# A recurrence and an MLP mixer on one core: another written-out order for all engines

## The chip, the core and the metric

The kernel runs on one core of a Trainium2 chip. The metric is the device time of one execution in microseconds (us). Before the change it is 173.35 us, the median of 3 runs (172.86 to 173.45). The engines are PE (TensorE), DVE (VectorE), ACT (ScalarE), POOL (GpSimd) and SP (SyncE).

## The reference

For each of 4 batches and 8 heads of 48 channels a gated recurrence runs over 768 steps. Its output, with the heads side by side (768 x 384), goes through an MLP mixer: first over the steps (token weights), then over the channels.

```python
f = 1.0 / (1.0 + np.exp(-f_logit))
for t in range(S):                       # S = 768
    state = f[:, :, t, :, None] * state + np.einsum('bhd,bhe->bhde', k[:, :, t], v[:, :, t])
    y[:, :, t] = np.einsum('bhd,bhde->bhe', q[:, :, t], state)
x = y.transpose(0, 2, 1, 3).reshape(B, S, H * D)
xt = x.transpose(0, 2, 1)
h = np.maximum(xt @ w_tok1, 0.0) @ w_tok2
u = x + h.transpose(0, 2, 1)
out = u + np.maximum(u @ w_ch1, 0.0) @ w_ch2
```

w_tok1 is 768 x 256, w_tok2 256 x 768, w_ch1 384 x 1536 and w_ch2 1536 x 384. All inputs and the output are float32; the kernel multiplies in bfloat16.

## The kernel before

**The recurrence by chunks.** The 768 steps of a batch are six chunks of 128. A name such as "sums 1 3" is the operation for batch 1, chunk 3. For each chunk ACT computes the logarithm of f from the loaded logits ("exp", "ln", L371 and L372); the logarithm is kept as a high bfloat16 part and a low part ("lo", L379, on DVE or POOL). PE sums both along the steps with a triangular matrix ("sums", L461 and L462). ACT takes the exponential of the sums both ways ("G", "Gi"), DVE multiplies q and k by them ("gated", L490), PE turns the products ("turn", L500), and DVE or ACT copies them out of PSUM ("turned"). PE multiplies them ("scores", L413), DVE masks the result ("masked", L541), and PE forms the part of the state that the chunk adds ("parts", L429). "tsum" and "state" (L577 for the decay) bring the state from one chunk to the next, and "spread" casts it to bfloat16 in two halves (L277 on ACT, L281 on POOL), which "y" of the next chunk multiplies (L560), before its own part within the chunk (L564). Batch 0 works by pairs of chunks instead, on a layout of its own: scores at L676, the masks at L706, "within" at L719, and y with the old state at L743; y 0 5 is the last of these.

**The mixer.** "tok1" (L757) takes the six chunks of x times w_tok1, "h1T" is its ReLU, "tok2" (L773) multiplies by w_tok2, and DVE adds x ("u"). u is turned, by PE ("ut" and its copy "uT") in batches 0 and 1 and by a transposing DMA of SP in batches 2 and 3. "ch1" (L826, three products of 384 columns) takes w_ch1, whose two halves are two tiles; "zT" is its ReLU on ACT (L357) or DVE (L359); "ch2" (L845, three groups of four products for each 128 rows) takes w_ch2; DVE adds u ("sum", L851) and SP stores.

**Loads.** SP loads f of batch 0. All other loads of q, k, v, f and the weights are DMAs that POOL issues (L266 and L272), among its arithmetic and in its row's order.

**What sets the order.** All operations of the four batches are first made as a list of some 1,050, each with what it needs. Then `Plan.run` walks the string ORDER and issues them in this order, so ORDER fixes the row of every engine. A number is an operation; a letter behind it chooses the engine where there is a choice (A for ACT, D for DVE, G for POOL); a number behind a colon chooses the PSUM bank, of which there are eight. `w512` and `w128` are idle products in float32, and `s11` is eleven idle products of 64 columns in bfloat16; their results are not used:

```python
if token[0] in "zsw":
    idle(int(token[1:]), {"z": 512, "s": 64, "w": 0}[token[0]])
    continue
...
op = self.ops[int(token)]
op.engine = engine or op.engines[0]
```

The text speaks of these numbers: 206 is y 0 5, 204 y 0 4, 358, 366, 394 and 402 are the sums of chunks 0 to 3 of batch 1, 208 to 213 and 215 to 220 the tok1 products of batch 0, 344 and 347 the low parts of chunks 1 2 and 1 3, 161 and 199 within of chunks 0 2 and 0 4, 170 and 201 the states 0 3 and 0 4, 62, 81 and 354 the loads of f for batches 1, 2 and 3, 46 and 47 the halves of w_ch1, and 48 w_ch2.

Of the kernel before, what the change touches and what calls it, by code (L numbers as in the profile page):

```python
# [33 lines left out]


ORDER = """
w512 w512 w512 s11 32 0G 6G 33 8G 20D 9D 5G 34 13D 7G 1 21G 35 2 24A 23A 27D 3A 37 26A 29D 14D 28 49 17D 36 19D 51 22G
38 50 53D 54 12D 39 52D 25D 55 100:0 15G 40 58 105:1 56D 57D 102 59 10G 137:2 104 41 11D 30D 107 114:3 60D 142:4 101 42
110 106 108 31A 103 62 119:1:0 139 18D 109 115 145 61D 111:5 143 112 125 144 180:6 141 138 147 113A 116D 43 151:2 146
126A 130 118:3:4 140 44 127A 117:5:1 123 182 152 175:0 153A 4G 122 45 121 176 131G 148:3 120 177 149 64 156:4:2 183 181  # L40
178 124:0:5 150A 162 63 184 186:6 179 187 185 132A 134 47 128D 154:3:4 188A 189:1 158 190 133G 191D 163G 66 157 165A
# [5 lines left out]
296:5 346 362 278:0 275A 347D 370 304:3 351 273D 277A 372:1 365D 279A 280:2 349 297D 298:0 271A 373D 350G 402:4 290:6
305D 75 292:5 281D 291A 374:3 299D 293A 78 375:6 352 376:2 386 403 286:5 76 377 404 284:6 378 79 264:0 258:7 379 285D 77
381A 262:3 259D 265A 282:6 263A 81 399 382:7 283A 300:0 385 287A 400:3 387 380A 302:5 407 405 384D 391:2 406 408:4 80
401D 393A 431:1 301A 409D 260:6 353G 303A 388D 410:0 261A 412:5 383A 414 411:6 389G 392A 268:7 415 434 413 266:2 435  # L50
390A 423 294:0 269A 419:3 416G 267D 433 462:7 87 439:6 424 420A 422 469:2 470 441 463 417G 288:5 421A 418G 432 464 83
471 289D 428:3 295A 311:1 429D 82 316:0 425D 430A 436 90 440 317 426A 442 318 85 472 312 86 313 93 465 437:6 314 91
443:3 319 438A 321:1 320 444D 96 447:0 445:5 99 446:4 448 322 450 427G 331:6 449 97 306:0 457 590 84 587 458 454:5 323
588 451G 455D 584 332 452G 324 585 453G 326:4 92 466 459:1 589G 327 460A 586G 328 89 467 473 474 468A 610:3 475D 461A
307 593 329 479:2 611 476:4 612 480 482:1 456A 485:7 477 596 481G 488:2 483 478A 308 94 486 594 602:1 489 484G 491:7 604
615 496:4 88 498:2 605 494:5 333 499D 497D 606 595G 613 495D 616:2 492 512:5 490G 487A 309 646:7 603 354 334 500:0 524:3
647 617D 513A 508:6 607 501A 510:5 591 525D 502:0 493A 608:1 511D 592G 599 506:3 503D 609D 504:0 95 528:5 507A 505D 509A
638:4 529D 597 522:0 639 618:5 598G 523D 640 619:6 648 620:3 630 98 641 534:0 623 544:6 629 642 600 625G 520:4 624G 614
545A 621 355 530:2 649 631 514:1 622 521A 675:7 531A 651 516:3 515A 643 518:2 601D 356 536:1 519A 635:4 677 537D 526:2
517A 535A 644:1 676 626:3 645D 652:0 628A 550:5 627A 527D 559:6 653D 632G 551A 678 683:2 634G 633G 656:5 679 818 655:7  # L60
659 654:3 684 650 560 660G 685 658 830 661G 542:2 667 662A 538:3 636A 666 637A 561 680 824 672:4 821 686 554:0 833 657
539A 552:7 668 831 673D 663:3 540:5 562 681:1 541A 713:6 819 714 682D 687:5 664A 555 820G 553A 688D 674A 556 669G 665A
357 834 691:4 557 689:3 671A 690:7 543A 693 564:0 827 692 670A 715 836:3 822 694 706:2 698:1 702 695G 548:4 699D 835G
696A 707 708 701 825 565 697G 839 700D 823G 532:7 840 837 716 703:1 533D 838 709 549D 546:5 704D 717 569:4 705D 710 718
843:1 719D 711 570 846 547D 712D 574:6 847 845 826D 844 720:2 828 841 723:5 729:1 848 870:3 721 829G 849 726:7 871 575
727 722G 735:2 724 842 732:7 736 725A 566 730 728A 737G 877:2 872 733 738 576 880 734G 912:7 731A 832G 571 873 739 852:1
572 878 579:5 567 879 905:4 855 330 882 580 857A 881 577 856G 913 874 581 863 914 875 851:1:6 582 850:7:2 907 886:0 876
861 756:5 864D 742:3 862 865G 762:6 743A 853 760:1 906 889 908 867:3 854 764:2 883 866A 780:4 757A 765D 890G 768:7 761A
763D 892G 772:2 310 910 769A 583 858:6 891A 758:1 335 773A 746:7 868A 315 859A 740:2 568 747D 781A 909 766:5 898 860A
741D 325 919:4 759A 899G 885:0:7 767A 884:6:2 897 776:1 888 754:5 750:0 887 784:6 751A 896 744:2 869A 785D 893:7 777D  # L70
902:3 911 901G 778:6 755D 900G 782:1 745D 779A 915 770:5 903A 573 894A 941:6 916 942 752:2 771A 786:0 753D 943 934:5 922
787A 748:2 783D 923G 944 813:0 749D 924G 904D 925G 935 774:2 895D 936 937 775A 803:7 917:2:3 918:1:4 921 804 929 805 920
808:4 806 926:3 930 809 927A 931:1 945 814 932A 946 938 939 947D 793:7 940A 928D 933A 810 954:1 963:3 960:5 964 957:6
788:2 965A 958 948:3 811 959G 789 961 949 951:4 962G 798:5 952 950A 967 799 955 794 956G 953G 795 966 800 815 812 790
807 563 1008:1 1014:4 1002:3 1015D 998:6 801 1003A 1004:4 791 988:5 816 1005A 992:2 999D 990:4 796 968:6 989D 797 991A
1010:7 1009A 802 993A 972:4 558 792 974:1 973D 817 1000:2 1011D 578 984:4 1001A 982:7 975A 994:2 978:1 996:5 979D 980:0
# [839 lines left out]
```

## Time and profile before

| | |
|---|---|
| median of 3 runs | 173.35 us (172.86 to 173.45) |
| the profiled execution | 173.47 us |
| its span (first to last instruction in the trace) | 171.7 us |
| mean granted clock of TensorE | 0.996 |
| loads and stores | 22.72 MB in DMA packets, 132 GB/s over the span |

In a row of the profile stand the start, the busy time, the engine, the line of kernel.py, the operation, what it writes and reads with the shapes, how many instructions it groups, and in brackets the engine's idle time ahead of it with what ended that. PE's product of 384 columns reads as some 0.326 us, but the products overlap, and one starts every 0.163 us. The issue of a load on POOL is a row of POOL; its landing is read from the DMA rows, whose last number is the time from issue to landing.

### The profile page before, as it was taken

Reading aid. Unit: us, or ns where it says so; the run is one execution under the profiler, and the core shown is the slowest. Engines: PE = TensorE matmul, PEld = TensorE weight load, DVE = VectorE, ACT = ScalarE, POOL = GpSimd, SP = SyncE. Lnnn points to the kernel's source line nnn. Section 1 sums busy time; section 2 is a strip of 40 time slices with the busy share of each in tenths; the row PEclk is TensorE's granted clock in tenths of the full one; section 3 lists DMA queues with packets and bytes.
Section 4 is the critical chain, followed back from the end, with each engine's and each line's share of the span. In section 5 each row is a group of like instructions: output and inputs, shape, how many; then the busy total and the mean of one; then the engine's idle time right before and its main releaser. Section 6 shows DMA issues by size and latency. Waiting matters only on the chain.

```text
span 171.7 us, 4436 instructions
## 1 busy us (share of the span) xinstructions
PE 162.2 (94%) x1753; PEld 103.2 (60%) x1753; DVE 123.3 (72%) x262; ACT 105.9 (62%) x240; POOL 90.8 (53%) x131
## 2 busy tenths in 40 slices
PE   6998688999999989999999999999999999999991
PEld 3476565666766645666757665565766656566660
DVE  5589986899995662999777889696976380754051
ACT  5999869995995615979898844959441420542000
POOL 8999678959959598897841933411220031000000
PEclk9999999999999999999999999999999999999998
DMA  5999999999999999969999190978370008250024
GB/s 143 226 171 223 202 196 189 185 144 171 185 196 188 148 139 52 56 83 214 106 143 79 8 130 7 189 166 239 111 168 4 0 7 242 96 211 0 0 96 181
DMA packets 89572, 22.72 MB, mean 132 GB/s; under 512 B 82288, under 2 KB 88736, under 8 KB 89552
## 3 DMA queue, kind: packets, MB, share of 16 engines
q0 software_dynamic: 69600, 13.77, 92.6%
q1 hardware_dynamic: 19952, 8.69, 19.1%
q8 instruction: 13, 0.21, 0.5%
q14 instruction: 7, 0.06, 0.1%
HBM read 25.17 MB, written 4.72 MB: 174 GB/s over the span
## 4 chain that ended last, share of the span: by engine, by line
PE 74%; POOL 11%; DMA 7%; ACT 3%; issue 2%; DVE 1%; POOLq 0%; DVEq 0%
PE ps L826 27%; PE ps L845 24%; DMA f_sb<-in_f_logit_dram 7%; PE ps L757 4%; PE ps L773 4%; POOL qk_sb L266 4%; PE ps L500 3%; PE ps L413 3%; POOL v_sb L266 2%; PE ps L564 2%; PE ps L429 2%; PE ps L461 2%; PE ps L462 2%; PE ps L560 1%; PE ps L811 1%
## 5 line engine op out<-in xcount | busy, mean ns | idle before, releaser
L826 PE MATMUL ps<-uT,w_ch 128*128 128x384 bf16 x288 | 52.6, 326 | 0.0
L845 PE MATMUL ps<-w_ch,zT 128*128 128x384 bf16 (+2 forms) x300 | 52.6, 320 | 0.0
L357 ACT ACTIVATE zT<-ps 128x384 bf16<-128x384 f32 x55 | 25.2, 491 | 21.5 <-PE ps L826 21.1
L845 PEld LDWEIGHTS <-zT 128*128 128x128 bf16 x300 | 27.7, 98 | 17.0
L826 PEld LDWEIGHTS <-w_ch 128*128 128x128 bf16 x288 | 26.8, 97 | 16.3
L359 DVE TENSOR_SCALAR zT<-ps 128x384 bf16<-128x384 f32 x41 | 21.4, 552 | 13.0 <-PE ps L826 12.6
L541 DVE TENSOR_TENSOR AmT<-ps,tri_bf 128x512 bf16<-128x512 f32 x36 | 23.4, 684 | 2.6 <-PE ps L413 2.4
L851 DVE TENSOR_TENSOR x_nat<-x_nat,ps 128x384 f32<-128x384 f32 (+2 forms) x25 | 12.8, 533 | 11.3 <-PE ps L845 11.1
L379 POOL TENSOR_TENSOR Llo<-L 128x384 bf16<-128x384 f32 x15 | 12.4, 834 | 11.8 <-ACT L L372 11.7
L266 POOL DMA_DIRECT2D qk_sb<-in_q_dram x16 | 15.7, 986 | 2.9 <-DMA f_sb<-in_f_logit_dram 2.3
L266 POOL DMA_DIRECT2D v_sb<-in_v_dram x16 | 15.8, 990 | 2.7 <-DMA f_sb<-in_f_logit_dram 1.7
L266 POOL DMA_DIRECT2D qk_sb<-in_k_dram x16 | 15.8, 990 | 0.0
L281 POOL CAST u_bf<-x_nat 128x384 bf16<-128x384 f32 x10 | 5.0, 508 | 14.6 <-issue 10.1
L277 ACT ACTIVATE x_bf<-ps 128x384 bf16<-128x384 f32 x15 | 7.0, 486 | 8.8 <-PE ps L564 8.8
L281 POOL CAST state_bd<-state 48x192 bf16<-48x192 f32 x22 | 8.0, 363 | 8.0 <-PE ps L560 3.0
L757 PE MATMUL ps<-x_bf,w_tok 128*128 128x384 bf16 x48 | 11.9, 326 | 0.0
L789 DVE TENSOR_TENSOR x_nat<-x_nat,ps 128x384 f32<-128x384 f32 x21 | 10.5, 546 | 1.6 <-PE ps L773 1.6
L490 DVE TENSOR_TENSOR qk<-qk_sb,GG 128x768 bf16<-128x768 bf16 x18 | 10.8, 615 | 0.0
L577 POOL TENSOR_TENSOR state<-tsum,glast 128x192 f32<-128x192 f32 x9 | 4.6, 507 | 10.4 <-PE ps L826 4.9
L471 ACT ACTIVATE GG<-ps 128x384 bf16<-128x384 f32 x18 | 8.9, 492 | 1.9 <-PE ps L462 1.0
L371 ACT ACTIVATE f_sb<-f_sb 128x384 f32<-128x384 f32 x18 | 9.1, 524 | 1.3 <-DMA f_sb<-in_f_logit_dram 1.2
L372 ACT ACTIVATE L<-f_sb 128x384 f32<-128x384 f32 x18 | 9.5, 526 | 0.2
(101 smaller groups left out, 264.3 us busy)
## 6 DMA issues: line engine op xcount, KB each, us to landing
out_dram<-x_nat SPq DMA_DIRECT2D x23, 192.0 KB, 2.4
f_sb<-in_f_logit_dram POOLq DMA_DIRECT2D x3, 1152.0 KB, 11.9
f_sb<-in_f_logit_dram SPq DMA_DIRECT2D x3, 384.0 KB, 4.0
qk_sb<-in_q_dram POOLq DMA_DIRECT2D x12, 96.0 KB, 7.7
qk_sb<-in_k_dram POOLq DMA_DIRECT2D x12, 96.0 KB, 7.2
w_ch<-in_moe_w_ch_dram POOLq DMA_DIRECT2D x2, 576.0 KB, 12.8
v_sb<-in_v_dram POOLq DMA_DIRECT2D x12, 96.0 KB, 7.5
w_ch<-in_moe_w_ch_dram POOLq DMA_DIRECT2D x1, 1152.0 KB, 10.4
```

The source lines that it names most:

```text
L266: lambda eng=eng, into=into, of=of: eng.dma_start(out=into, in_=of),
L281: nc.gpsimd.tensor_copy(out_, in_)
L357: nc.scalar.activation(out_, in_, AF.Relu, bias=0.0, scale=1.0)
L359: nc.vector.tensor_scalar(out_, in_, 0.0, None, ALU.max)
L379: op.fn = lambda: (nc.vector if op.engine == DVE else nc.gpsimd).tensor_tensor(lo, full, hi, ALU.subtract)
L490: add(("gated", b, c, *names), DVE, lambda n=n: nc.vector.tensor_tensor(qk[it][:, n, :, 0:D], qk_sb[nb][:, n, :, c, :], GG[i][:, n], ALU.m ...
L541: add(("masked", b, c, p), DVE, lambda half=half, made=made: nc.vector.tensor_tensor(half, made(), tb4, ALU.mult), need=["tri_bf"], make=[ ...
L757: add(("tok1", b, rt, kt), PE, lambda rt=rt, kt=kt, pm=pm: nc.tensor.matmul(banks[pm.at][:, 0:DM], lhsT=w_tok1[:, kt, rt * 128:(rt + 1) * ...
L789: nc.vector.tensor_tensor(to, un, banks[pm.at][:, 0:DM], ALU.add)
L826: nc.tensor.matmul(banks[pm.at][:, 0:384].rearrange("p (n t) -> p n t", t=128), lhsT=w[:, kt, c0:c0 + 128], rhs=uT[:, rows3, kt, :], start ...
L845: nc.tensor.matmul(banks[pm.at][:, 0:n1 - n0], lhsT=zT[:, kt, tt * 128:(tt + 1) * 128], rhs=w_ch2[:, kt, n0:n1], start=(kt == 0), stop=(kt ...
L851: add(("sum", b, tt, n0), DVE, lambda un=un, pm=pm, n=n1 - n0: nc.vector.tensor_tensor(un, un, banks[pm.at][:, 0:n], ALU.add), make=[("x_n ...
```

## The change

Only the string ORDER is replaced. The operations, what they compute and the code that makes them stay. The new order differs from the first line to the last; its first lines and those around the sums of batch 1 read:

```diff
-w512 w512 w512 s11 32 0G 6G 33 8G 20D 9D 5G 34 13D 7G 1 21G 35 2 24A 23A 27D 3A 37 26A 29D 14D 28 49 17D 36 19D 51 22G
...
-193:3:6 136A 169 155:1:4 135A 164G 197 67 192:2:5 159 46 160 336 195 w512 w128 161:4:6 170G 337 196 339 338G 173 198 340
-166 194:2 172A 341G 199:5:1 129A 200 171A 68 174A 204 201D 358:0 342 167D 208:2 203A 209 202G 205D 215:3 359 65 206 210
-361 211 207D 216 212 217 343 213 218 219 214D 360 220 344G 366:7 168D 221A 242 238 369 230:2 69 231 222:4 223 232 367
...
+w512 w512 w384 s19 32 20G 7G 33 8D 6G 10D 0D 34 11G 19D 1 5D 9G 2 24D 3A 27D 23A 18D 21G 22G 35 49 37 50 16G 51 36 52D
...
+129A 169 193:1:5 164A 160 135A 47 128D 165A 192:4:6 159 339 65 336 197 161:2:0 337 170G 195 340 166 338G 198 342 194:5
+173 172A 196 171G 358:1 343 341G 200 199:6:7 360 167D 359 201G 215:5 136D 204 361 216 203G 366:4 205D 202G 208:3 362
+174A 217 68 363 209 206 367 210 168D 364:1 369 67 207D 211 218 345 212 365D 213 66 219 220 214A 374:2 221D 368 242 72
...
```

- **Idle products.** Before: three w512 and eleven small ones at the start, and w512 and w128 between the scores 0 4 and within 0 2. Now: two w512, one w384 and nineteen small ones at the start, and none later.
- **Engines.** DVE has 281 operations instead of 261, ACT 225 instead of 239, POOL 121 instead of 127. The ReLU copies zT stand at 48 on ACT and 48 on DVE instead of 55 and 41, the casts x_bf at 6 and 18 instead of 15 and 9, the low parts at 13 on DVE and 11 on POOL instead of 9 and 15, and the casts of the state at 16 on ACT and 24 on POOL instead of 18 and 22.
- **Rows.** Every engine's row has another order, the loads on POOL too. y 0 5 (206) now stands behind five tok1 products (208, 209, 215, 216, 217) and the sums of 1 0 and 1 1 (358, 366); before it stood behind three (208, 209, 215) and the sums of 1 0.

POOL's row shows the three places that the prediction speaks of. The first is the end of the startup. Before, the row goes from the load of q 1 1 to the cast of state 0 4; state_95 is the state, Llo_79 the low parts, w_ch10_66 and w_ch11_67 the halves of w_ch1.

```order
L266 DMA qk_sb1_70<-in_q_dram 128x8x48
L272 DMA w_ch10_66<-in_moe_w_ch1_dram 128x3x768
L577 TENSOR_TENSOR state_95<-tsum_96,gpair1_121 128x192
L379 TENSOR_TENSOR Llo_79<-L1_78 128x8x48 x2
L266 DMA v_sb1_73<-in_v_dram 128x8x48
L281 CAST state_bd0_97<-state_95 48x4x48
```

Now, from the first half of w_ch1 on, with the load of v 1 0 ahead of state 0 3:

```order
L272 DMA w_ch10_66<-in_moe_w_ch1_dram 128x3x768
L272 DMA w_ch11_67<-in_moe_w_ch1_dram 128x3x768
L266 DMA v_sb1_73<-in_v_dram 128x8x48
L577 TENSOR_TENSOR state_95<-tsum_96,gpair1_121 128x192
L379 TENSOR_TENSOR Llo_79<-L1_78 128x8x48
L281 CAST state_bd1_98<-state_95 48x4x48
L379 TENSOR_TENSOR Llo_79<-L1_78 128x8x48
L577 TENSOR_TENSOR state_95<-tsum_96,gpair0_120 128x192
L281 CAST state_bd0_97<-state_95 48x4x48 x2
```

State 0 4 has moved here from DVE, both halves of its cast stand here, one half of the cast of state 0 3 has moved here from ACT, and no load stands among them any more.

The second place is the stretch of loads that follows, up to w_ch2. Before, one low part stands in it, that of chunk 1 2; that of 1 3 is on DVE.

```order
L266 DMA v_sb1_73<-in_v_dram 128x8x48
L379 TENSOR_TENSOR Llo_79<-L1_78 128x8x48
L266 DMA qk_sb1_70<-in_k_dram 128x8x48
L266 DMA qk_sb1_70<-in_q_dram 128x8x48
L266 DMA v_sb1_73<-in_v_dram 128x8x48
L266 DMA qk_sb1_70<-in_q_dram 128x8x48
L288 MEMSET grow1_93 32x512
L266 DMA qk_sb1_70<-in_k_dram 128x8x48
L266 DMA v_sb1_73<-in_v_dram 128x8x48
L272 DMA w_ch2_68<-in_moe_w_ch2_dram 128x12x384
```

Now both are in POOL's row, that of 1 2 behind four loads and that of 1 3 behind three more:

```order
L266 DMA v_sb1_73<-in_v_dram 128x8x48
L266 DMA qk_sb1_70<-in_q_dram 128x8x48
L266 DMA qk_sb1_70<-in_k_dram 128x8x48 x2
L379 TENSOR_TENSOR Llo_79<-L1_78 128x8x48
L266 DMA qk_sb1_70<-in_q_dram 128x8x48
L266 DMA qk_sb1_70<-in_k_dram 128x8x48
L266 DMA qk_sb1_70<-in_q_dram 128x8x48
L379 TENSOR_TENSOR Llo_79<-L1_78 128x8x48
L272 DMA w_ch2_68<-in_moe_w_ch2_dram 128x12x384
```

The third place is where the state of batch 1 is cast for y 1 4 (state_bd1) and y 1 5 (state_bd0), among the loads of batch 2. Before, six loads stand ahead of the first of these casts, and two more between it and state 1 4:

```order
L266 DMA qk_sb2_71<-in_k_dram 128x8x48
L266 DMA qk_sb2_71<-in_q_dram 128x8x48
L266 DMA v_sb2_74<-in_v_dram 128x8x48
L266 DMA qk_sb2_71<-in_k_dram 128x8x48
L266 DMA v_sb2_74<-in_v_dram 128x8x48 x2
L281 CAST state_bd1_98<-state_95 48x4x48
L266 DMA qk_sb2_71<-in_k_dram 128x8x48
L266 DMA v_sb2_74<-in_v_dram 128x8x48
L577 TENSOR_TENSOR state_95<-tsum_96,glast2_90 128x192
L281 CAST state_bd0_97<-state_95 48x4x48 x2
```

Now state 1 3 and the first half of its cast stand ahead of three loads, the other half behind them, and the cast for y 1 5 behind two more and the load of f for batch 3, which before came later:

```order
L577 TENSOR_TENSOR state_95<-tsum_96,glast1_89 128x192
L281 CAST state_bd1_98<-state_95 48x4x48
L266 DMA v_sb1_73<-in_v_dram 128x8x48
L266 DMA qk_sb2_71<-in_k_dram 128x8x48
L266 DMA qk_sb2_71<-in_q_dram 128x8x48
L281 CAST state_bd1_98<-state_95 48x4x48
L266 DMA v_sb2_74<-in_v_dram 128x8x48 x2
L266 DMA f_sb1_76<-in_f_logit_dram 128x48x48
L281 CAST state_bd0_97<-state_95 48x4x48
```

The load of f for batch 2 (81) has also moved: it now stands behind the load of k 1 4, and those of k 1 5, q 1 5 and v 1 4, which were ahead of it, behind it.

More of the change, by code (lines that the diff above doesn't have):

```diff
@@ L36 @@
 ORDER = """
-w512 w512 w512 s11 32 0G 6G 33 8G 20D 9D 5G 34 13D 7G 1 21G 35 2 24A 23A 27D 3A 37 26A 29D 14D 28 49 17D 36 19D 51 22G
[L38 to L41, printed above, removed]
@@ L42 @@
-193:3:6 136A 169 155:1:4 135A 164G 197 67 192:2:5 159 46 160 336 195 w512 w128 161:4:6 170G 337 196 339 338G 173 198 340
-166 194:2 172A 341G 199:5:1 129A 200 171A 68 174A 204 201D 358:0 342 167D 208:2 203A 209 202G 205D 215:3 359 65 206 210
-361 211 207D 216 212 217 343 213 218 219 214D 360 220 344G 366:7 168D 221A 242 238 369 230:2 69 231 222:4 223 232 367
-226:3 227 73 243 224 368 234 250:0 244A 228 235 239 245A 246:7 71 251D 247A 363 248:1 394:0 237A 249D 70 364:7 236A 233
-256:1 240A 225 252:6 16G 272:2 345 241D 72 396 276:4 253D 348 254:5 257D 270:6 397 74 255D 229 274:1 398 395 371 48
@@ L47 @@
[L47 to L76, printed above, removed]
@@ L77 @@
-985D 997A 970:1 983A 995D 986:4 969D 1041:2 1012:6 1006:7 976:5 1007D 1036:3 971D 977A 987A 1013D 1046:7 1042 981A 1043
-1026:0 1044 1031:6 1047 1037 1048 1027 1021:2 1032 1033 1022 1034 1038 1035 1045 1028 1039 1023 1049 1029 1050 1016:7
-1040 1024 1017 1025 1030 1018 1019 1020
+w512 w512 w384 s19 32 20G 7G 33 8D 6G 10D 0D 34 11G 19D 1 5D 9G 2 24D 3A 27D 23A 18D 21G 22G 35 49 37 50 16G 51 36 52D
+54 14D 13D 25D 12D 53G 26A 55 28 39 100:0 58 56D 105:1 40 57D 102 59 38 104 137:2 101 60D 142:3 42 108 107 61D 106 110
@@ new lines @@
+41 139 109 119:1:0 144 103 114:4 29D 143 62 111:5 125 138 115 112 116D 180:1 113A 130 146 126A 140 117:0:4 30A 127G
+148:5 43 31A 149 141 175:2 181 147 121 145 150A 131G 118:3:6 120 44 151:0 176 123 156:5:4 182 17G 152 177 122 15G 153A
+185 63 124:2:3 179 184 183 134 133A 178 189:6 64 132A 190 162 186:1 191A 187 4G 154:5:0 45 157 188A 163G 158 155:6:0 46
+129A 169 193:1:5 164A 160 135A 47 128D 165A 192:4:6 159 339 65 336 197 161:2:0 337 170G 195 340 166 338G 198 342 194:5
+173 172A 196 171G 358:1 343 341G 200 199:6:7 360 167D 359 201G 215:5 136D 204 361 216 203G 366:4 205D 202G 208:3 362
@@ new lines @@
+174A 217 68 363 209 206 367 210 168D 364:1 369 67 207D 211 218 345 212 365D 213 66 219 220 214A 374:2 221D 368 242 72
+238 377 243 239 222:5 244D 234 241A 344G 235 226:1 240A 378 227 256:4 236A 230:3 70 254:6 257D 231 245A 228 252:2 394:4
+255A 69 253D 223 346 248:7 232 290:6 249A 224 73 288:2 396 229 291A 284:7 233 347G 250:1 286:6 285A 251D 351 48 246:3
+402:1 397 247D 300:7 225 76 352 289D 270:3 405 301D 264:5 74 272:2 406 237A 348 296:7 71 370 273D 268:0 349 398 271D 75
+265A 292:2 269D 297A 276:3 371 287A 266:7 350D 403 258:6 353D 395 298:0 267A 81 277D 404 262:4 293A 372:3 439:2 373D
@@ new lines @@
+382:1 260:7 299D 79 375:5 261A 376:0 386 259A 78 304:7 263A 407 302:5 385 441 294:4 384A 379 280:6 295A 383D 381G 274:3
+440 380G 387 278:4 399 431:0 281D 388G 282:2 432 275D 391:6 279A 469:1 283A 400:3 393D 433 408:4 392A 77 326:2 390A 409D
+434 306:6 389G 303D 435 401D 327 305D 410:5 411:0 413 412:7 328 415 414 470 321:3 416D 436 417A 307 423 418G 82 437:5
+424 419:0 329 462:7 83 422 322 421A 330 438A 420D 308 425G 427G 463 323 80 445:0 324 85 587 331:4 449 596 332 584 86 309
+585 464 448 310 428:6 426G 590 311:0 87 429D 333 442 430A 84 586D 593 443:5 588 334 354 447:6 444D 602:3 454:4 605 450
@@ new lines @@
+471 451D 446:2 606 589D 594 316:6 604 457 312 452G 603 89 458 453A 610:5 591 607 472 465 88 611 459:2 595D 612 608:3
+592D 455A 313 613 460D 466 615 473 597 474 456D 467 646:5 468A 598G 475D 317 647 314 609A 479:1 91 461D 482:7 488:0 480
+649 476:2 483 616:4 481G 648 477 491:1 484G 599 638:7 489 95 478A 496:2 492 485:5 640 318 497D 617A 92 486 498:2 494:1
+620:0 490G 499A 495D 618:5 319 600 90 619:1 622 493A 508:2 96 520:6 623 509A 630 518:5 639 601G 621 830 528:2 641 510:1
+631 487G 521D 506:0 642 624G 821 629 625G 526:6 614 507A 94 519D 522:7 824 643 502:0 831 93 524:5 527D 529A 512:4 833
@@ new lines @@
+503D 97 635:2 818 513D 514:0 511A 98 819 504:4 516:6 505D 834 820D 644:1 356 517A 515D 500:4 525A 626:3 675:6 651 501A
+554:5 678 637D 548:4 636D 679 677 652:0 632G 645D 628A 650 555 355 827 523D 676 653D 559:2 549A 627D 634A 546:6 656:4
+547A 655:3 633G 659 825 654:7 822 836:6 657 556 823G 666 683:1 667 560 660G 685 832G 828 658 552:0 839 532:3 557 99
+536:7 680 661A 684 713:5 662G 561 553A 686 838 542:1 537D 357 672:0 562 544:7 668 673D 663:2 545A 687:4 669D 543A 665D
+843:7 837 538:1 674D 826G 846 533D 530:6 847 845 671G 714 534:3 531D 844 840 681:0 688D 539A 535A 706:7 707 664D 550:1
@@ new lines @@
+682D 540:2 551A 691:3 541A 689:6 694 690:1 670A 693 870:2 695G 574:3 692 873 697G 575 696G 702 874 829G 576 701 841 715
+708 698:4 577 871 877:1 835D 709 703:3 848 569:0 699D 849 878 570 704D 872 700D 716 717 710 842 718 711 905:4 719D 712A
+852:2 705A 732:5 558 855 879 735:7 320 880 856G 723:3 736 563 729:6 857A 726:1 733 881 737G 908 571 730 325 724 579:5
+731A 863 734A 720:3 727 564:2 739 875 565 721 906 882 907 851:3:1 315 725A 850:6:7 722G 861 886:4 728A 566 862 738 580
+854 581 864D 876 567 865A 867:6 572 866A 772:2 889 869A 853 883 786:0 912:3 773D 787A 770:7 890D 913 578 582 758:0 891G
@@ new lines @@
+335 898 892G 858:2 759A 764:5 909 899D 914 859D 766:4 568 868A 765D 754:3 771A 910 752:6 755A 767D 941:7 768:5 753A 915
+860A 885:4:3 769D 884:6:0 919:2 897 782:1 888 742:5 744:4 887 750:6 922 896 784:0 751A 893:2 743D 746:6 911 901G 778:5
+747A 740:3 785A 895A 902:6 900A 942 894D 808:0 916 783A 923G 745D 934:2 762:1 924G 741D 925G 935 583 904D 756:4 763A
+760:3 757A 943 779A 780:1 761D 774:5 903D 776:3 775D 788:6 781D 777A 917:5:4 918:1:3 921 936 809 930 813:5 920 810 929
+944 926:4 931:3 927D 748:1 932A 811 937 945 933D 946 938 803:0 947A 928A 939 749A 798:7 940D 793:1 948:2 951:4 954:3 952
@@ new lines @@
+804 955 953G 799 949 956A 963:3 950A 957:2 964 814 966 965G 794 815 789 960:3 790 961 805 958 962A 816 959A 972:2 974:5
+967 800 980:3 573 801 988:4 812 791 981A 976:7 817 975A 806 984:6 807 795 802 994:0 796 985A 1014:5 995D 797 982:1 989D
+1006:0 983D 978:4 977D 996:1 1010:7 990:6 1011D 992:3 991D 968:7 997D 993A 1004:6 979D 1012:1 1005D 970:4 1015D 998:6
+969D 986:5 973D 1002:7 999D 1000:2 971D 1003A 1008:6 1007D 987A 1046:7 1013D 1031:5 1001D 1036:1 1009D 1037 1041:6
+1021:2 1047 1032 1048 1022 1038 1023 1039 1042 1049 1024 1050 1043 792 1026:2 1040 1016:7 1033 1017 1034 1027 1044 1035
@@ L80 @@
+1045 1028 1025 1018 1029 1030 1019 1020
 """
```

## The prediction

> **What bounds the kernel now.** I read the page's busy shares and its chain first, then the windows, then the timelines of PE and POOL. The windows give length, then the busy time (instructions) of PE, PEld, DVE, ACT and POOL, then TensorE's granted clock, the DMA share and GB/s.
>
> ```profile
> span 171.7 us, 4436 instructions
> PE 162.2 (94%) x1753; PEld 103.2 (60%) x1753; DVE 123.3 (72%) x262; ACT 105.9 (62%) x240; POOL 90.8 (53%) x131
> PE 74%; POOL 11%; DMA 7%; ACT 3%; issue 2%; DVE 1%; POOLq 0%; DVEq 0%
> ...
> 0.00:7.23 7.23, 5.78 (x18) 2.28 (x18) 3.67 (x15) 5.12 (x10) 6.62 (x18) 1.00 0.91 187
> 7.23:27.84 20.61, 17.39 (x425) 12.73 (x423) 17.90 (x42) 18.19 (x41) 18.03 (x26) 1.00 1.66 194
> 27.84:61.14 33.30, 33.16 (x353) 21.73 (x351) 28.32 (x59) 26.47 (x61) 27.32 (x33) 1.00 1.91 176
> 61.14:65.24 4.10, 3.02 (x39) 2.01 (x37) 1.66 (x3) 0.00 (x0) 3.93 (x8) 1.00 2.24 119
> 65.24:168.14 102.90, 102.82 (x936) 64.42 (x931) 71.24 (x143) 56.16 (x130) 34.95 (x50) 1.00 0.76 102
> 168.14:170.42 2.28, 0.01 (x1) 0.00 (x0) 0.56 (x1) 0.00 (x0) 0.00 (x0) 1.00 0.58 217
> ```
>
> PE is the bound, at 94%, and from 27.84 us on it hardly stops: 33.16 of 33.30 us, then 102.82 of 102.90. The two kernels issue the same products, apart from the idle ones, so a list can win only where PE stands. There are three such places: the head up to 7.23 us, where PE runs idle products; the startup from 7.23 to 27.84, busy 17.39 of 20.61 (1.35 of this with idle products, below); and the 4.10 us at 61.14, busy 3.02. The last product ends at 168.14; two sums, the store and the end of the program fill 3.6 us behind it, and the changed list ends in the same way. The profiled run took 173.47 us, 1.77 more than its span and 0.12 above the median of 173.35; my sum starts from 173.47.
>
> **The change, step by step.**
>
> *Head.* The idle products change in number, but the first real one is the sums of chunk 0, which need the loads of f and their exponentials. These keep their places: no gain, no loss; the row of 0 to 7.23 us gives what it is worth, and I see nothing that moves its end by over 0.1.
>
> *Startup.* Where it ends is set by the last product with the state (y 0 5), at 27.67:
>
> ```profile
> 20.39 0.42 PE L676 MATMUL ps<-zT 48*64 48x128 bf16 x16 [0.91 <-DVE zT L279]
> ...
> 21.59 1.35 PE L877 MATMUL ps<-x_nat 128*128 128x512 f32 x4
> 22.87 0.89 PE L719 MATMUL ps<-v_sb,zT 64*128 64x48 bf16 x32
> ...
> 27.67 0.33 PE L743 MATMUL ps<-state_bd,zT 128*128 128x96 bf16 x4 [0.38 <-POOL state_bd L281]
> ```
>
> It waits for POOL's cast of the state. POOL's own rows say why that is late:
>
> ```profile
> 22.66 0.88 POOL L266 DMA_DIRECT2D qk_sb<-in_q_dram  x1 [2.30 <-DMA f_sb<-in_f_logit_dram]
> 23.53 0.74 POOL L272 DMA_DIRECT2D w_ch<-in_moe_w_ch_dram  x1
> 24.29 0.52 POOL L577 TENSOR_TENSOR state<-tsum,gpair 128x192 f32<-128x192 f32 x1
> 24.76 1.61 POOL L379 TENSOR_TENSOR Llo<-L 128x384 bf16<-128x384 f32 x2
> 26.31 0.94 POOL L266 DMA_DIRECT2D v_sb<-in_v_dram  x1
> 27.26 0.36 POOL L281 CAST state_bd<-state 48x192 bf16<-48x192 f32 x1
> ```
>
> A load's issue stood 2.30 us because the load of f 1, eight loads before it in POOL's row, had not landed. The same shows below at 57.91. I read from it that POOL has at most eight loads outstanding, and that the ninth holds all that is queued behind it. The changed row meets this wait too: the load eight behind f 1 is now v 1 0, with both weight halves issued ahead of it. It starts at the same 22.66, and then: .88 load, .52 state 0 3 (24.06), .81 low part of chunk 1 0 (24.87), .36 cast (25.23), .81 low part of 1 1 (26.04), .52 state 0 4, two casts of .36: 27.28. So y 0 5 starts near 27.34 instead of 27.67, and ahead of it PE has by then done two more tok1 products (2 x .16) and the sums of 1 1 (.33). Gain .33 + .33 + .33 = 1.0; I take **-0.9**. From below it is nothing, if DVE's masks end later than I count; no part of this stretch allows more than the 3.2 us that PE stood.
>
> *The idle products taken out* (1.35 us at 21.59) stood in time in which PE waited for DVE's masks, which still last: the product behind them started as the masks were done. Cover: the masks. Price if nothing else moves: 0. But those four products also kept PE busy, and the clock is read from here:
>
> ```profile
> 17.00:20.40 3.40, 2.26 (x72) 1.65 (x62) 3.34 (x9) 3.12 (x6) 3.14 (x6) 1.00 1.03 208
> 20.40:23.80 3.40, 3.19 (x87) 2.19 (x88) 3.40 (x7) 2.14 (x6) 1.14 (x2) 1.00 1.59 191
> ...
> 167.01:170.42 3.41, 1.14 (x7) 0.49 (x5) 0.56 (x1) 0.00 (x0) 0.00 (x0) 1.00 0.63 233
> 170.42:171.70 1.28, 0.00 (x0) 0.00 (x0) 0.00 (x0) 0.00 (x0) 0.00 (x0) 0.50 0.00 0
> ```
>
> After 3.4 us with 1.14 us of products the grant fell to 0.50; after 3.4 us with 2.26 us it did not. Without the idle products the stretch from 20.40 has 3.19 - 1.35 = 1.84 of 3.40, between the two and nearer 2.26. Both ends are kept: 0, or the price worked out as the second rival. The Trainium skill, page "TensorE: Matmul & The Clock Gate", section "What's actually happening", speaks against this edit: the clock is halved after an idle window of some 3.4 us, and the windows run free of the kernel. The grant's fall 2.3 us after the last product agrees with a window fixed in time; how much work makes a window idle, no row here shows between 1.14 and 2.26. By that page the sum would be the same unless one window holds next to nothing.
>
> *A wait that is added.* The low part of chunk 1 3 goes from DVE to POOL, behind the load of q 1 3. That load is the eighth after the second weight half, which now follows the first at once:
>
> ```profile
> w_ch<-in_moe_w_ch_dram POOLq DMA_DIRECT2D x1, 576.0 KB, 13.9
> ...
> w_ch<-in_moe_w_ch_dram POOLq DMA_DIRECT2D x1, 576.0 KB, 11.7
> qk_sb<-in_q_dram POOLq DMA_DIRECT2D x1, 96.0 KB, 9.8
> ```
>
> Before, the first half was issued at 17.20 and landed at 31.1; q 1 1, issued at 22.66, landed at 32.5 with another load of its size between, thus .7 each; the other half, issued at 23.53, landed at 35.3, thus 2.8. Now the halves land at about 31.1 and 33.9. The issue of q 1 3 waits until 33.9 or a little more, takes .88, the low part .81: 35.6 to 36.1. PE has 7.3 us of products from y 0 5 to the sums of 1 3: 31 of 384 columns and the two of the sums of 1 2 at .163 (5.4), 18 single transposes at .056 (1.0), and a turn of eight (.45), a score and y 0 5 (.45 together).
>
> ```profile
> 28.00 1.48 PE ps L757 x9
> ...
> 37.35 0.45 PE ps L500 x8
> ...
> w_ch<-in_moe_w_ch_dram POOLq DMA_DIRECT2D x1, 1152.0 KB, 10.4
> ```
>
> The nine at 1.48 are .164 each, the eight transposes .056 each. So PE arrives at 27.34 + 7.3 = 34.7 and stands until about 35.6 to 36.1. From 0 (POOL reaches the load early and the half lands by 33) to 1.5; I take **+0.9**, the near end. Behind the waiting load stand only the next low part and the load of the last weight, and that weight: issued near 36, with the 10.4 us of the row it lands by 47, and its first product stands 14 us of products behind the sums of 1 3, at 49.
>
> *58 to 65 us.* PE stood at two casts of the state:
>
> ```profile
> PE ps L560 <- POOL state_bd L281: 1.1, 2, 0.7
> ...
> 58.99 2.15 PE L845 MATMUL ps<-w_ch,zT 128*128 128x384 bf16 x12
> 61.83 0.33 PE L560 MATMUL ps<-state_bd,qkT 128*128 128x96 bf16 x4 [0.68 <-POOL state_bd L281]
> ...
> 64.15 0.33 PE L757 MATMUL ps<-x_bf,w_tok 128*128 128x384 bf16 x1
> 64.87 0.33 PE L560 MATMUL ps<-state_bd,qkT 128*128 128x96 bf16 x4 [0.39 <-POOL state_bd L281]
> ```
>
> ```profile
> 57.91 0.88 POOL L266 DMA_DIRECT2D v_sb<-in_v_dram  x1 [1.74 <-DMA f_sb<-in_f_logit_dram]
> 58.78 0.90 POOL L266 DMA_DIRECT2D qk_sb<-in_k_dram  x1
> 59.64 1.78 POOL L266 DMA_DIRECT2D v_sb<-in_v_dram  x2
> 61.38 0.40 POOL L281 CAST state_bd<-state 48x192 bf16<-48x192 f32 x1
> ```
>
> Twelve products from 58.99 end their slots at 60.95 and the next starts at 61.83: .88. One at 64.15 ends at 64.31, the next starts at 64.87: .56. Together 1.44. POOL was held 1.74 us for the load of f 2, and four loads of .88 stood between that and the cast. In the changed list f 2 is issued three chunk loads earlier (3 x .7 = 2.1, landing near 55.4 instead of 57.6), the load eight behind it is q 2 1, and POOL's half of the cast for y 1 4 stands right behind that. POOL comes to it at 57 to 58, so the cast is done by about 59, ahead of the 60.95 at which PE asks. The cast for y 1 5 has two chunk loads and the issue of f 3 ahead of it, until about 63.3: ahead of 64.3. Gain **-1.4**; from below -0.5, if the second cast comes late again.
>
> *The rest of the list*, 103 us at full rate, is the same work in another order. It can only lose. DVE takes 20 operations more in all, ACT 14 and POOL 6 fewer, and most of the difference falls early:
>
> ```profile
> 60.00:70.00 10.00, 8.93 (x75) 5.46 (x73) 5.29 (x11) 4.15 (x11) 8.85 (x14) 1.00 1.59 93
> 70.00:80.00 10.00, 9.99 (x108) 6.50 (x107) 9.64 (x22) 8.72 (x21) 8.78 (x11) 1.00 0.80 113
> ```
>
> DVE ran 33 operations in these 20 us, 14.93 us. By their places in the changed list 42 stand beside the same products: 19.0 us at the same mean (.452), 21 at .5. DVE is then full for 20 us, and what it does late PE awaits. From 0 to +1.6; I take **+0.5**.
>
> Sum: -0.9 + 0.9 - 1.4 + 0.5 = -0.9, from 173.47: 172.6, and 172.5 beside the median of the runs.
>
> **Rivals.** *Both gains, no new wait*: if the second weight half lands by 33 and DVE's queue absorbs its 42 operations, -0.9 - 1.4 = -2.3, 171.2. For it: PE has products from other chunks to run meanwhile. Against it: POOL's row alone, without any wait, brings the load of q 1 3 near 33.4.
>
> *The clock falls*: if the stretch around 20 to 24 us counts as idle, the next 3.41 us run at half speed. In 3.41 us at half speed at most half the work, 1.7 us, is left over, and PE is close to busy there: +1.7. With the forecast's -0.9 this is 174.2, slower. It decides between 1.14 and 2.26 us of products in one window. For it: 1.84 is the sum above, and a gap of 2 us is in it; windows that start elsewhere may hold 1.3. Against it: 1.84 is nearer to 2.26.
>
> *The gains are given back*: the change doesn't do what it says, as the waits on loads move to other places (the low part of 1 3, 1.4; a full DVE, 1.0). -0.9 - 1.4 + 1.4 + 1.0 = 0.1: about 173.5, and with 1.5 and 1.6 174.3.
>
> **How the numbers follow.** Forecast .41 (own range 171.8 to 172.8); both gains .12; clock .15 (slower); gains given back .32, of which .20 within 0.3% and .12 slower. 0.3% of 173.35 is 0.52 us, about what a measurement of this kernel can tell from no change. Faster .41 + .12 = .53; same .20; slower .15 + .12 = .27. The range runs from 171.0 (both gains and .2 elsewhere) to 174.6 (the clock's case, or all losses with a little over).
>
> **What would show it.** Right: y 0 5 near 27.3 behind two more tok1 products; POOL's load before the low part of 1 3 with a wait on the weight half, and PE standing near 35 for the low part; no wait of PE on the state's cast between 58 and 65, and POOL held for f 2 less than 0.5 us. Wrong: a granted clock of 0.5 anywhere between 20 and 30 us; waits of PE on DVE of more than 1 us between 60 and 85; or a wait on a load of batch 2 or 3, all of which I count as landed in time.

## The result and the profile after

The changed kernel takes 172.06 us (median of 20 executions) against 173.26 for the kernel before beside it (20 executions): ratio 0.9937, 95% interval 0.9914 to 0.9960. That is 1.1 us less (0.7 to 1.5). The forecast was 172.5, with a range of 171.0 to 174.6.

The page of the changed kernel, and windows of it cut where the granted clock changes (length; busy time of PE, PEld, DVE, ACT, POOL; clock; DMA share; GB/s):

```profile
span 169.8 us, 4441 instructions
PE 161.6 (95%) x1757; PEld 103.9 (61%) x1757; DVE 130.1 (77%) x282; ACT 101.1 (60%) x226; POOL 86.7 (51%) x125
PEclk9999956999999999999999999999999999999998
PE 88%; ACT 5%; DVE 2%; DMA 2%; issue 0%; DVEq 0%
```

```profile
18.20:21.61 3.41, 1.93 (x65) 1.39 (x63) 2.54 (x7) 3.37 (x8) 3.35 (x7) 1.00 1.32 195
21.61:25.02 3.41, 3.14 (x73) 2.44 (x73) 3.41 (x7) 3.10 (x8) 2.87 (x6) 0.50 1.93 177
25.02:28.44 3.42, 3.42 (x45) 1.89 (x43) 2.38 (x6) 2.50 (x6) 3.30 (x6) 0.50 1.23 210
28.85:166.23 137.38, 137.38 (x1315) 87.75 (x1312) 108.47 (x224) 76.40 (x174) 60.01 (x79) 1.00 1.12 121
```

Two things stand out. In the sixth and seventh slice of the page TensorE's clock is half for 6.83 us, behind a window in which PE ran 1.93 us of products. And from 28.85 us to its last product PE reads as busy without a break. POOL has gone from the chain (11% before) and PE's share is up from 74% to 88%. The last product ends at 166.23 instead of 168.14, the span is 1.9 us shorter; this execution took 172.62 us, 2.8 outside its span instead of 1.8, so the medians are the better measure.

The end of the startup, PE's row and then POOL's:

```profile
20.13 0.42 PE L676 MATMUL ps<-zT 48*64 48x128 bf16 x16 [0.86 <-DVE zT L706]
...
26.66 0.53 PE L743 MATMUL ps<-state_bd,zT 128*128 128x96 bf16 x4
...
28.68 0.33 PE L743 MATMUL ps<-state_bd,zT 128*128 128x96 bf16 x4
...
36.33 0.34 PE L461 MATMUL ps<-L,tri_bf 128*128 128x384 bf16 x1
```

```profile
22.44 0.92 POOL L266 DMA_DIRECT2D v_sb<-in_v_dram  x1 [0.53 <-DMA f_sb<-in_f_logit_dram]
...
26.28 0.74 POOL L281 CAST state_bd<-state 48x192 bf16<-48x192 f32 x2
...
34.22 0.88 POOL L266 DMA_DIRECT2D qk_sb<-in_q_dram  x1 [1.10 <-DMA w_ch<-in_moe_w_ch_dram]
35.11 0.84 POOL L379 TENSOR_TENSOR Llo<-L 128x384 bf16<-128x384 f32 x1
```

POOL does what was worked out: the casts for y 0 5 are done at 27.02 (27.28 forecast), the load of q 1 3 waits for the weight half until 34.22 (33.9), the low part of 1 3 is done at 35.95 (35.6 to 36.1). PE does not: y 0 5 starts at 28.68, later than before (27.67), and without waiting for POOL. So PE also comes late to the sums of 1 3, at 36.33, when the low part is there. Around 60 us no wait on a cast is left:

```profile
60.16 0.33 PE L560 MATMUL ps<-state_bd,qkT 128*128 128x96 bf16 x4
...
62.95 0.33 PE L560 MATMUL ps<-state_bd,qkT 128*128 128x96 bf16 x4
```

### The profile page after: what moved, and what is told of

Read it like the earlier page. It is cut to its first block, busy times and chain, and to the rows that moved or that the text cites. A ratio compares the mean times of both kernels' runs of the same rounds, so it can differ in the third digit from the quotient of the medians.

```text
span 169.8 us, 4441 instructions
## 1 busy us (share of the span) xinstructions
PE 161.6 (95%) x1757; PEld 103.9 (61%) x1757; DVE 130.1 (77%) x282; ACT 101.1 (60%) x226; POOL 86.7 (51%) x125
## 4 chain that ended last, share of the span: by engine, by line
PE 88%; ACT 5%; DVE 2%; DMA 2%; issue 0%; DVEq 0%
PE ps L826 28%; PE ps L845 28%; PE ps L757 5%; PE ps L773 5%; PE ps L500 3%; PE ps L413 3%; PE ps L461 2%; PE ps L564 2%; DMA f_sb<-in_f_logit_dram 2%; PE ps L462 2%; PE ps L429 2%; PE ps L560 2%; DVE zT L706 1%; PE ps L644 1%; PE ps L719 1%; ACT f_sb L392 1%
## 5 line engine op out<-in xcount | busy, mean ns | idle before, releaser
L826 PE MATMUL ps<-uT,w_ch 128*128 128x384 bf16 x288 | 52.0, 326 | 0.0
L357 ACT ACTIVATE zT<-ps 128x384 bf16<-128x384 f32 x48 | 22.3, 491 | 20.6 <-PE ps L826 16.8
L359 DVE TENSOR_SCALAR zT<-ps 128x384 bf16<-128x384 f32 x48 | 24.8, 550 | 2.8 <-PE ps L826 2.7
L757 PE MATMUL ps<-x_bf,w_tok 128*128 128x384 bf16 x48 | 13.0, 340 | 0.0
L279 DVE CAST x_bf<-ps 128x384 bf16<-128x384 f32 x18 | 9.9, 552 | 3.7 <-ACT x_nat L277 1.7
L281 POOL CAST u_bf<-x_nat 128x384 bf16<-128x384 f32 x8 | 4.3, 544 | 16.2 <-issue 11.4
L471 ACT ACTIVATE GG<-ps 128x384 bf16<-128x384 f32 x18 | 8.7, 489 | 5.2 <-DVE qk L490 3.6
L490 DVE TENSOR_TENSOR qk<-qk_sb,GG 128x768 bf16<-128x768 bf16 x18 | 10.0, 556 | 0.3 <-ACT GG L471 0.3
L773 PE MATMUL ps<-h1T,w_tok 128*128 128x384 bf16 x48 | 9.8, 326 | 0.0
L473 ACT ACTIVATE GG<-ps 128x384 bf16<-128x384 f32 x18 | 8.8, 491 | 1.6 <-PE ps L462 1.2
L379 POOL TENSOR_TENSOR Llo<-L 128x384 bf16<-128x384 f32 x10 | 8.3, 833 | 2.0 <-ACT L L372 2.0
```

The lines of the kernel that those rows point to most:

```text
L281: nc.gpsimd.tensor_copy(out_, in_)
L357: nc.scalar.activation(out_, in_, AF.Relu, bias=0.0, scale=1.0)
L359: nc.vector.tensor_scalar(out_, in_, 0.0, None, ALU.max)
L490: add(("gated", b, c, *names), DVE, lambda n=n: nc.vector.tensor_tensor(qk[it][:, n, :, 0:D], qk_sb[nb][:, n, :, c, :], GG[i][:, n], ALU.m ...
L757: add(("tok1", b, rt, kt), PE, lambda rt=rt, kt=kt, pm=pm: nc.tensor.matmul(banks[pm.at][:, 0:DM], lhsT=w_tok1[:, kt, rt * 128:(rt + 1) * ...
L773: nc.tensor.matmul(banks[pm.at][:, 0:DM], lhsT=w_tok2[:, kt, tt * 128:(tt + 1) * 128], rhs=h1T[:, kt, :], start=(kt == 0 and not held), st ...
```

## The experiments

Two theories. **Clock theory:** the idle products that the change took out had kept the clock up; in the changed kernel a window of the startup holds too few products, the clock falls for one or two windows, and what the new order wins in the startup is lost there. **Rival:** in the startup PE waits for DVE and POOL anyway, so its clock does not matter, and the time came out as it did for the reasons of the prediction. All ratios are to the kernel before on the same chip.

### The changed kernel again

No edit.

> The changed kernel once more, for its granted clock in each execution. Clock theory: the mean clock varies from execution to execution, between about 0.976 (two windows of 3.41 us at half speed in the startup) and 0.99, since the window's phase against the kernel is not fixed; executions at 0.976 take 0.5 to 1.0 us more than those at 0.99. Rival (PE waits for other engines in the startup whatever its clock): no difference of time between the two kinds above 0.2 us. Both: ratio to before about 0.994.

171.40 us, ratio 0.9919 (0.9902 to 0.9936). The trace of this execution has one window at half clock instead of two, and PE comes to the sums of 1 3 earlier:

```profile
19.65:23.06 3.41, 1.47 (x52) 1.02 (x53) 3.30 (x7) 3.36 (x8) 2.67 (x5) 1.00 1.53 184
23.06:26.47 3.41, 3.41 (x89) 2.53 (x88) 3.41 (x7) 3.09 (x8) 3.28 (x6) 0.50 1.83 182
```

```profile
27.91 0.33 PE L743 MATMUL ps<-state_bd,zT 128*128 128x96 bf16 x4
...
35.56 0.34 PE L461 MATMUL ps<-L,tri_bf 128*128 128x384 bf16 x1
36.16 0.32 PE L462 MATMUL ps<-Llo,tri_bf 128*128 128x384 bf16 x1 [0.26 <-POOL Llo L379]
```

y 0 5 is at 27.91, and now PE does wait for the low part, 0.26 us. Of the 20 executions of the result, 12 have a mean clock of 0.985 or 0.99 (median 171.7 us) and 8 one of 0.976 to 0.979 (median 172.5): the second window costs 0.7 us. No execution reached 0.996, which the kernel before has in most of its executions (table below). The clock does matter.

### Idle products back, and one load moved: the two edits and both

The first edit puts idle products where PE waited for the masks. The second moves the load of q 1 3 (73) behind the low part of 1 3 (347), which then no longer stands behind a wait for a weight half:

```diff
-154:5:0 45
+154:5:0 w256 45
...
-193:1:5 164A
+193:1:5 w128 164A
...
-192:4:6 159
+192:4:6 w128 159
```

```diff
-73 288:2 396 229 291A 284:7 233 347G 250:1
+288:2 396 229 291A 284:7 233 347G 73 250:1
```

> The changed kernel with idle products again between the masks of the startup (w256 behind scores 0 2, w128 behind scores 0 5 and behind scores 0 4, where PE waited 0.9, 0.5 and 0.8 us). Clock theory: no half clock before the end, mean clock 0.990 to 0.996; y 0 5 near 27.5 instead of 28.68; but PE then comes to the sums of 1 3 at about 35.0 and waits there 0.6 to 1.0 us for the low part, so that only 0.2 to 0.5 us are left in the time: about 171.6. Rival: clock up, but y 0 5 where it was (28.4 to 28.7) and the time that of the changed kernel, 172.0.

> The changed kernel with one token moved: the load of q 1 3 behind the low part of chunk 1 3 on POOL, so that the low part no longer stands behind a wait for the second half of w_ch1. As the prediction had it (PE waits 0.9 us for this low part): 0.9 us faster, 171.1. Clock theory: where the clock fell, PE comes to the sums of 1 3 so late (36.3) that the low part is there already, and nothing changes; only executions whose clock stayed up gain, 0.3 us on the median at most.

> Both edits. Clock theory: y 0 5 near 27.5, no wait at the sums of 1 3, PE busy from there to the end: 0.9 to 1.3 us faster than the changed kernel, about 171.0, ratio to before 0.986 to 0.989. Rival: as the changed kernel, 172.0; if the prediction's wait alone counts, as the kernel with the one token moved.

| kernel (one chip) | median, us | ratio, 95% interval | mean clock of its executions |
|---|---|---|---|
| before | 172.95 | 1 | 0.996 or more in 12 of 15 |
| changed | 171.40 | 0.9919 (0.9902 to 0.9936) | none above 0.99 |
| idle products back | 171.43 | 0.9917 (0.9892 to 0.9942) | 0.996 or more in 4 of 6 |
| load moved | 172.05 | 0.9940 (0.9918 to 0.9963) | none above 0.99; 5 of 10 at 0.977 or less |
| both | 170.29 | 0.9848 (0.9835 to 0.9861) | 0.998 or more in 4 of 4 |

Neither edit alone gains anything, both together 1.1 us. With the idle products alone the clock stays up in four of six executions. In the profiled one, which is one of the four, y 0 5 comes at 26.93, 0.98 us earlier than in the trace above, and PE gives 0.7 of this back at the low part, behind which it goes on at 35.86 instead of 36.16:

```profile
18.25:21.67 3.42, 2.98 (x69) 2.14 (x70) 2.52 (x7) 3.38 (x8) 3.37 (x7) 1.00 1.31 191
21.67:25.08 3.41, 3.06 (x80) 2.07 (x79) 3.41 (x7) 3.30 (x8) 3.05 (x6) 1.00 1.94 178
```

```profile
26.93 0.33 PE L743 MATMUL ps<-state_bd,zT 128*128 128x96 bf16 x4
...
34.67 0.33 PE L461 MATMUL ps<-L,tri_bf 128*128 128x384 bf16 x1
35.86 0.32 PE L462 MATMUL ps<-Llo,tri_bf 128*128 128x384 bf16 x1 [0.85 <-POOL Llo L379]
```

This is the wait that the prediction had worked out (PE at 34.7, some 0.9 us of waiting). With both edits the low part is early and PE runs through:

```profile
33.40 0.85 POOL L379 TENSOR_TENSOR Llo<-L 128x384 bf16<-128x384 f32 x1
```

```profile
35.01 0.34 PE L461 MATMUL ps<-L,tri_bf 128*128 128x384 bf16 x1
35.18 0.32 PE L462 MATMUL ps<-Llo,tri_bf 128*128 128x384 bf16 x1
35.34 1.95 PE L826 MATMUL ps<-uT,w_ch 128*128 128x384 bf16 x11
```

The rival falls. The load moved alone was to bring 0.9 us by the prediction's wait and next to nothing by the clock theory; it brought none. It even came out 0.65 us above the changed kernel, with intervals that overlap. Its clock was the lower one in more of its executions, but those at 0.986 or 0.99 also took longer (171.9 us on the median of five, against 171.4 of four), so a part of the 0.65 stays open.

### The kernel before without its idle products

```diff
-336 195 w512 w128 161:4:6
+336 195 161:4:6
```

> The kernel before without its two idle products between scores 0 4 and within 0 2. Clock theory: the window there loses 1.3 of its 2.3 to 3.2 us of products, the clock falls to 0.5 for one or two windows in most executions (mean clock 0.976 to 0.99), and the time grows by 0.3 to 1.0 us: 173.2 to 173.9, ratio 1.002 to 1.006. Rival, as the prediction's sum had it (idle products stand in idle time and cost and bring nothing): 172.9, ratio 1.000.

173.49 us against 172.96, ratio 1.0018 (0.9987 to 1.0050). The clock fell in all 12 executions (0.98 or less); the kernel before beside it had 0.996 or more in 20 of 29. So these products do hold the clock, but in this order the price, 0.5 us on the median, is not clear of noise, and the time alone doesn't decide between the two expectations.

### Casts moved in the kernel before

This takes the gain between 58 and 65 us by itself. The first edit moves POOL's half of the cast for y 1 4 (427) ahead of four loads; the second moves state 1 4 and the cast for y 1 5 (451 to 453) too:

```diff
-450 427G 331:6
+450 331:6
...
-86 313 93
+86 427G 313 93
```

```diff
-449 97 306:0
+449 451G 452G 453G 97 306:0
...
-588 451G 455D 584 332 452G 324 585 453G 326:4
+588 455D 584 332 324 585 326:4
```

> The kernel before with one cast moved: POOL's half of the cast of state 1 3 (for y 1 4) ahead of four loads instead of behind them. Queue theory: the first wait of PE (0.88 us at 60.95) goes, but the cast for y 1 5 stays behind the same loads, so PE, which is earlier now, waits there 1.1 us instead of 0.56: 0.3 to 0.4 us faster, ratio 0.998. Rival (the waits are independent): 0.9 us faster, ratio 0.995.

> As the last one, and state 1 4 with both halves of its cast ahead of two more loads. Queue theory: both waits go, 1.44 us faster: 171.5, ratio 0.992. Rival (the gain of the changed list between 58 and 65 us comes from the earlier landing of f 2, or is lost again further down): less than half of that.

One cast: 172.77 us, ratio 0.9986 (0.9962 to 1.0010). Both: 172.94 us, ratio 0.9984 (0.9956 to 1.0012). Neither is clear of noise. For the one cast the rival's 0.995 lies outside the interval, as the queue theory had it; for both casts the queue theory's 0.992 lies outside, and the 1.44 us are not there. The executions with both fall into two groups: six at a clock of 1.0, 172.1 to 172.8 us, and five at 0.99 or less, 173.1 to 173.9 (a twelfth, at 0.99, took 174.7). The profiled one is of the first group:

```profile
27.79 0.33 PE L743 MATMUL ps<-state_bd,zT 128*128 128x96 bf16 x4 [0.38 <-POOL state_bd L281]
...
61.10 0.33 PE L560 MATMUL ps<-state_bd,qkT 128*128 128x96 bf16 x4
...
63.59 0.33 PE L560 MATMUL ps<-state_bd,qkT 128*128 128x96 bf16 x4
```

There both waits are gone. Where the startup ends late, it seems, there is nothing to gain; the next two runs look at that.

### The kernel before again

No edit.

> The kernel before, unchanged, for a second trace of it. Landing theory (the 1.44 us of waits at 58 to 65 us were in part an accident of the one profiled execution, in which f 2 landed at 57.63; in the three later traces of kernels with the same row of loads it landed at 56.6 to 56.9): f 2 lands near 56.7, POOL is held for it under 0.8 us, and PE's two waits there come to 0.4 to 0.8 us together; span near 171.1. Rival (the waits are as the first trace shows, and the moved casts gain little since the time is lost again later): f 2 near 57.6 and 1.44 us of waits.

> The same kernel once more, a third trace: as the last one, by both theories.

The first execution, 173.15 us (clock 0.998), PE's row and POOL's:

```profile
27.91 0.33 PE L743 MATMUL ps<-state_bd,zT 128*128 128x96 bf16 x4 [0.38 <-POOL state_bd L281]
...
59.24 2.15 PE L845 MATMUL ps<-w_ch,zT 128*128 128x384 bf16 x12
61.52 0.33 PE L560 MATMUL ps<-state_bd,qkT 128*128 128x96 bf16 x4
...
63.84 0.33 PE L757 MATMUL ps<-x_bf,w_tok 128*128 128x384 bf16 x1
64.56 0.33 PE L560 MATMUL ps<-state_bd,qkT 128*128 128x96 bf16 x4 [0.39 <-POOL state_bd L281]
```

```profile
57.61 0.88 POOL L266 DMA_DIRECT2D v_sb<-in_v_dram  x1 [1.20 <-DMA f_sb<-in_f_logit_dram]
...
63.78 0.73 POOL L281 CAST state_bd<-state 48x192 bf16<-48x192 f32 x2
```

The second, 173.05 us (clock 0.990: one window fell):

```profile
28.64 0.34 PE L743 MATMUL ps<-state_bd,zT 128*128 128x96 bf16 x4
...
61.98 0.33 PE L560 MATMUL ps<-state_bd,qkT 128*128 128x96 bf16 x4
...
64.47 0.33 PE L560 MATMUL ps<-state_bd,qkT 128*128 128x96 bf16 x4
```

POOL was held for f 2 1.74 us in the first trace of this kernel, 1.20 here, and not at all in the second of these. PE's two waits, counted as in the prediction from the ends of the slots of 0.163 us, were 1.44, then 0.88 (61.20 to 61.52 and 64.00 to 64.56), then nothing. So neither theory fits both executions: the hold and the waits differ from execution to execution.

The better reading is that y 1 5 starts at 64.87, 64.56 and 64.47, nearly at one time, though y 0 5 came at 27.67, 27.91 and 28.64. In the first two POOL's chain of loads and casts holds y 1 5 back. In the third PE comes to it by itself, after the casts are done at 64.06 (63.33, and 0.73 for the two). A startup 0.7 us later is paid with a wait that is not there. The executions beside these runs say the same: seven of the kernel before with a clock of 0.986 to 0.99 took 172.96 us on the median, twenty with 0.997 or more 172.94. With the casts moved y 1 5 comes at 63.59 in place of 64.56 after nearly the same startup (27.79 and 27.91), 1.0 us, and only then does the startup show in the time.

### Further than the change

The kernel with both edits of above is taken on: y 0 5 (206) goes behind two more tok1 products (210, 211), called af_y5 below; then the idle products become bfloat16 of 512 columns (`z2` for `w256`, `z1` for `w128`):

```diff
-209 206 367 210 168D
+209 210 211 206 367 168D
...
-207D 211 218
+207D 218
```

> The kernel with both edits of the changed one (idle products back, the load of q 1 3 behind the low part), and y 0 5 behind two more tok1 products, as PE waited 0.42 us for the cast ahead of y 0 5. If the cast alone delays PE there: 0.33 us faster, 169.95, ratio to before 0.983. Rival: the wait only moves to the tok1 product of chunk 5 or to h1T behind it, 170.3 as without the edit.

> As af_y5, but the idle products in the startup are bfloat16 of 512 columns (two, one and one) instead of float32. If dense products keep the clock up better than the float32 ones, no execution falls: clock at 0.997 or more in all, 170.0 with a narrow spread. If the kind of product doesn't matter, as af_y5: a part of the executions at 0.99, with 0.6 us more.

> af_y5 once more, beside the last one: 170.0 to 170.1 where the clock stays up, 170.7 where one window fell, median 170.2.

af_y5: 170.25 us, ratio 0.9838 (0.9803 to 0.9873), and once more, on another chip, 170.66, ratio 0.9872 (0.9829 to 0.9916); with the bfloat16 ones 170.33, ratio 0.9845 (0.9810 to 0.9879). None differs clearly from the two edits alone (0.9848). In executions with a clock of 0.997 or more af_y5 takes 170.1 on the median of seven, where the two edits alone took 170.2 to 170.4: some 0.1 to 0.2 us of the 0.33, but on other chips, on which the kernel before differs by as much (172.95, 172.96 and 173.32), so that this gain is not shown. In all three the clock fell in a part of the executions, two or three of six; so few show no difference between the kinds of product. The four executions of the two edits in which it stayed up were thus too few to say that it always does. The kernel with the two edits beats both kernels, and nothing tried behind it is shown to be better.

## Why the prediction came out right, point by point

The time lies in the range and the sign is right. The sum is right by errors that cancel, and so by luck.

- **Startup, -0.9.** Failed. Between the two profiled executions y 0 5 is 1.0 later with 0.67 us of products more done ahead of it: +0.3. In the second trace of the changed kernel, with one window at half clock, it is 0.24 later: -0.4. What was worked out of POOL's row was right (without the fall: 26.93, 0.74 earlier, and 0.67 more done, -1.4); the price of the idle products was not. "Price if nothing else moves: 0" left out that they held the clock, and the prediction's own sign of being wrong, a granted clock of 0.5 between 20 and 30 us, came in both traces. The rival that had the fall got 0.15 with its time of 174.2, while the fall itself is in every execution of the changed kernel. Its price of 1.7 us is what two windows cost, not one: against the kernel with idle products y 0 5 comes 1.75 us later with two windows at half clock and 1.0 with one (26.93, 28.68, 27.91). With the load moved, where no wait hides it, taking the idle products out costs 1.8 us on the medians (170.29 and 172.05). In the changed kernel the wait for the low part (below) hides the first window; the second costs the 0.7 us of above.
- **The clock's windows.** One reading was off. Counted back from 170.42 in steps of 3.413 us, the window that held its clock is not 17.00 to 20.40 with 2.26 us of products but 16.82 to 20.24 with 2.43, and the next one, 20.24 to 23.65, has 3.05, or 1.70 without the idle products.
- **The wait that is added, +0.9.** Right as a mechanism (0.85 of idle time with the clock up), hidden in the result by the late startup: 0 in the first trace, 0.26 in the second. The two errors belong together: the fall of the clock takes up time that PE would have spent waiting for the low part.
- **58 to 65 us, -1.4.** The waits went, as forecast. But 1.44 us was the reading of one execution; by the same count it was 0.88 (0.32 and 0.56) and 0 in two others. The moved casts gain 1.0 us of it between two traces in which the clock stayed up. On the medians they gain 0.6 where it stayed up (172.37 of six executions against 172.94 of twenty) and nothing to be measured where it fell (173.2 of five against 173.1 of nine).
- **The rest, +0.5.** Wrong in sign. DVE ran 43 operations beside the products of 60 to 80 us, as counted (42), and was nearly full, but PE waited for none:

```profile
60.00:70.00 10.00, 10.00 (x114) 6.52 (x113) 9.86 (x22) 8.00 (x17) 8.57 (x10) 1.00 1.42 169
70.00:80.00 10.00, 10.00 (x114) 6.83 (x113) 9.34 (x21) 9.56 (x23) 9.59 (x16) 1.00 1.62 98
```

From y 0 5 to the end of the last product the changed kernel takes 137.55 us (28.68 to 166.23); the kernel before, in the execution that has no wait on a cast, takes 139.09 (28.64 to 167.73). Of these 1.54 us, 0.67 are the products done earlier. For the other 0.87, five starts in that trace of the kernel before are late against the usual distance between two such starts, by 0.14 to 0.35 us and 1.05 together: a product of ut (L811) at 33.25, a turn at 71.88, a y at 91.46, and tok2 at 105.95 and 106.42. In the changed kernel no start behind y 0 5 is late by over 0.13. What held the five was not tested, and why the new order has none like them stays open.
- **Sum.** In the two profiled executions +0.3, 0 and -1.4 leave -0.8 of the -1.9 for the rest; on the medians the whole is -1.2. The prediction came to -0.9.

Before, two paths stood near balance: a late startup was hidden by POOL's casts at 64 us. The change took that second path away and put a nearer one in its place, the low part of 1 3 near 36 us. With the clock up PE waits there for what the startup won; with one window at half clock it waits a little, and with two not at all, and then it runs without a wait from y 0 5 on.

## What to carry to other kernels

An idle product that costs nothing may still earn something: before it is taken out, count the products left in each stretch as long as the clock's window, at its worst place, and test that in several executions. Where a stage ends by the later of two paths, one edit alone shows nothing; make both, and look at more than one trace before pricing a wait of a microsecond. What one edit wins ahead of a fixed landing is waited for there, so the next wait must be worked out from the gain, not from the old trace.
